# A small load of the output weights split in two: 112 rows, and 16 rows read as 4 groups of 4

## The chip, the core and the metric

The kernel runs on one core of a Trainium2 chip. The metric is the device time of one execution in microseconds (us); the kernel before took 375.05 us, the median of 3 runs (374.96 to 375.16). Besides the compute engines (PE for matmuls, DVE, ACT and POOL for the rest) the core has 16 DMA engines, which move data between the chip's memory and the core's own memory. The compute engines and SP issue loads; the 16 engines carry them out.

## What is computed

One decoding step of attention over a long cache, gated by a small bilinear network:

```python
xn = _layernorm(x, axis=-1)
s = _A_ref(xn, A_k_cache, A_v_cache, A_wq, A_wo)
g = _silu(_B_ref(xn, B_w_gate, B_w_up, B_w_down))
return x + s * g

# _A_ref, cut: 16 query heads share 8 cached heads, 4096 keys of 256, batch 2
scores = jnp.einsum("bhqd,bhkd->bhqk", q, k) * (Dh ** -0.5)
p = _softmax(scores, axis=-1)
o = jnp.einsum("bhqk,bhkd->bhqd", p, v)
return o.reshape(B, Sq, Hq * Dh) @ wo

# _B_ref, cut
h = jnp.einsum("bsd,df->bsf", x, w_gate) * jnp.einsum("bsd,df->bsf", x, w_up)
return jnp.einsum("bsf,fd->bsd", h, w_down)
```

All numbers are 32-bit floats. The caches are 134 MB of the 158.5 MB that are read; each byte is used once.

## The kernel before

The host lays every input out as 128 rows, one for each partition of the core's memory, so that a load is 128 contiguous rows and nothing is rearranged on the way.

**Stages.** First the gating network: `w_gate` and `w_up` come into `low`, `w_down` into `buf1`, `wq` into `buf0`. Then the 16 pairs of cached head and batch follow, two large buffers in turn; each load of the loop (L130) brings 64 KB a partition, the values of one pair beside the keys of the next. The last two pairs' values come as two loads of 32 KB a partition (L133).

**The output weights.** `wo` is 32 steps; a step is a [128, 448] block, 1792 bytes a partition, and is multiplied with a piece of the attention's result (`oT`). The steps come in six loads (L134 to L138): 14, 9 and 4 steps (`ABREAST`) into `low`, then 3, 1 and 1 (`DIRECT`) into the upper half of `buf1`. Each has its own semaphore, `wo0` to `wo5`.

**The order of the loads.** SP issues nearly all loads, one after the other, into one queue (`dma_side`). It waits only until a buffer is free: before L133 until PE is done with a pair, and before the fourth load of `wo` until PE is done with another. What is issued early waits in the queue behind what is in it already. Two small loads are issued by ACT: `x` (2 rows, L162), and `xo`, x again (8 rows, L164).

**The end of the program.** PE waits for each load of `wo` in turn (L438). The first 27 steps accumulate in `o`, four abreast (L322); ACT copies that to `ys` (L196). The last 5 steps go straight to `acc` (L446), and `spread` (L326) adds `ys` to it. Then DVE multiplies with the gate (L295) and adds x (L298), and SP stores the result (L140):

```python
        for n, lo, hi in zip(won, bounds, bounds[1:]):
            e.wait_ge(n, 16)
            for i in range(lo, hi):
```

A load's semaphore reaches 16 when all of its data has landed, so PE goes on when the last of the DMA engines that carry that load is done.

Of the kernel before, what the change touches and what calls it, by code (L numbers as in the profile page):

```python
# [8 lines left out]
B, D = 2, 448  # L9
# [15 lines left out]
WO = 4 * HKV  # L25
ABREAST = (14, 9, 4)
DIRECT = (3, 1, 1)


class Queue:  # L30
# [20 lines left out]
        self.e.wait_ge(sem, n).then_inc(sem, -n)  # L51


def program(nc, known, x, xo, wgu, wd, wq, kv, vv, wo, out):
    def sb(name, shape):
        return nc.alloc_sbuf_tensor(name, shape, F32).ap()

    def ps(name, shape):
        return nc.alloc_psum_tensor(name, shape, F32).ap()

    first = nc.alloc_semaphore("first")
    sems = {n: nc.alloc_semaphore(n) for n in (
        "x", "xg", "gu", "wd", "wq", "k0", "k1", "v14", "v15", "t0", "t1", "pt", "sr", "ob", "q", "m", "mx", "res")}
    won = [nc.alloc_semaphore(f"wo{i}") for i in range(len(ABREAST + DIRECT))]
    pe = Queue(nc, nc.tensor, "pe", known)
    dv = Queue(nc, nc.vector, "dv", known)
# [14 lines left out]
    xg, gate, sig, r0, r1 = (sb(n, [128, SL]) for n in ("xg", "gate", "sig", "r0", "r1"))  # L81
# [8 lines left out]
    m = sb("m", [128, 2])  # L90
    mx = sb("mx", [1, NT, W])
    p = sb("p", [128, 2, 512])
    su = sb("su", [128, 2])
    sr = sb("sr", [128, 128])
    r = [sb(f"r{i}i", [128, REP]) for i in range(2)]
    pT = sb("pT", [128, 2, BLK, 128])
    ob = sb("ob", [128, 512])
# [4 lines left out]
    pt = [ps(f"pt{i}", [128, NK, 128]) for i in range(2)]  # L102
# [5 lines left out]
    bounds = [0]  # L108
    for n in ABREAST + DIRECT:
        bounds.append(bounds[-1] + n)  # L110
    early = bounds[len(ABREAST)]

    def wo_step(i):
        return low[:, i * D:(i + 1) * D] if i < early else late[:, (i - early) * D:(i - early + 1) * D]
# [4 lines left out]
    def dma_side():  # L119
        e = nc.sync  # L120
        for lo, hi in zip(GU, GU[1:]):
            e.dma_start(low[:, lo:hi], wgu[:, lo:hi]).then_inc(sems["gu"], 16)
        e.dma_start(buf[1][:, :14 * D], wd).then_inc(sems["wd"], 16)
        e.dma_start(buf[0][:, :28 * 512], wq).then_inc(sems["wq"], 16)
        sp.after(pe, "y4")
        for h in range(2):
            e.dma_start(buf[1][:, h * ROW:(h + 1) * ROW], kv[0][:, h * ROW:(h + 1) * ROW]).then_inc(sems[f"k{h}"], 16)
        for i in range(N - 2):
            sp.after(pe, *(("q", 1) if i == 0 else ("s", 1) if i == 1 else ("v", i - 2)))
            e.dma_start(buf[i % 2], kv[1 + i]).then_inc(turns[i % 2], 16)  # L130
        sp.after(pe, "v", N - 4)
        for h in range(2):
            e.dma_start(buf[0][:, h * ROW:(h + 1) * ROW], vv[h]).then_inc(sems[f"v{N - 2 + h}"], 16)  # L133
        for n, lo, hi in zip(won, bounds, bounds[1:]):  # L134
            if lo == early:
                sp.after(pe, "v", N - 3)
            t = low[:, lo * D:hi * D] if hi <= early else late[:, (lo - early) * D:(hi - early) * D]
            e.dma_start(t, wo[:, lo * D:hi * D]).then_inc(n, 16)  # L138
        sp.after(dv, "res")
        e.dma_start(out, r1).then_inc(sems["res"], 16)  # L140
        e.wait_ge(sems["res"], 16)
        last = nc.alloc_semaphore("last")
        e.sem_clear(range(first.num, last.num + 1))
# [156 lines left out]
    def pe_side():  # L300
        e = nc.tensor
# [18 lines left out]
        def abreast(t, lhs, rhs, i, total):  # L320
            c = i % NT
            return e.matmul(t[W * c:W * (c + 1), :D], lhs, rhs, start=i < NT, stop=i >= total - NT)  # L322

        def spread(start, stop):
            for c in range(NT):
                ins = e.matmul(acc[W * c:W * (c + 1), :SL], pick.rearrange("p b j -> p (b j)"),  # L326
                               ys[:, c * SL:(c + 1) * SL], start=start, stop=stop)
            return ins
# [104 lines left out]
        def left(i):  # L433
            g, j = divmod(i, 4)
            return oT[g][:, j // 2, j % 2].rearrange("p b j -> p (b j)")

        for n, lo, hi in zip(won, bounds, bounds[1:]):
            e.wait_ge(n, 16)  # L438
            for i in range(lo, hi):
                if i >= 4 * (HKV - 1):  # L440
                    pe.after(dv, "oT", N - 1)
                if i < early:
                    ins = abreast(o, left(i), wo_step(i), i, early)
                else:
                    for c in range(NT):
                        ins = e.matmul(acc[W * c:W * (c + 1), :SL], left(i), wo_step(i)[:, c * SL:(c + 1) * SL],  # L446
                                       start=lo == early and i == lo, stop=i == WO - 1)
            if hi == early:
                pe.ev(ins, "w4")
            if lo == early:  # L450
                pe.after(ac, "accs")
                spread(False, False)
# [3 lines left out]
    act_side()  # L456
    dve_side()
    dma_side()
    pe_side()
    return {q.name: q.at for q in (pe, dv, ac, po, sp)}  # L460

# [44 lines left out]
```

## Time and profile before

| | |
|---|---|
| median of 3 runs | 375.05 us |
| the profiled execution's own time | 375.17 us |
| its span, first instruction to last | 373.9 us |
| PE busy | 243.6 us (65%) |
| DVE, ACT, POOL busy | 60.3, 45.7, 5.0 us |
| mean granted TensorE clock | 0.79 of full speed |

The profile is that of one execution; its times count from the first instruction, and the 1.3 us between span and time lie around it. Busy shares are means over stages. What sets the end is read from the chain of waits, and how evenly the 16 DMA engines are loaded from the DMA share of short windows: it is the mean over the 16, so that a share of 0.50 late in the program is 8 engines at work. A 1/16 is 0.06.

### The profile page before, as it was taken

What the parts mean: (1) busy time and instruction counts of PE and PEld (TensorE: products, weight loads), DVE (VectorE), ACT (ScalarE), POOL (GpSimd) and SP (SyncE); (2) the same over time, 40 slices, a digit from 0 to 9 for tenths busy, and PEclk for the clock granted to TensorE, in tenths of its full rate; (3) what the DMA queues carried; (4) which work ended last, traced back from release to release, by engine and by line L of the source; (5) the groups of instructions that cost most, each with busy time, mean ns of one, the idle gap of its engine ahead of it and who ended that gap; (6) DMA issues with size and microseconds to landing.
All of it is one profiled execution on the core that took longest, in us unless ns stands there. A gap on an engine that the chain in (4) does not pass through costs nothing. (4 is left out here: it accounts for less than half of the span.)

```text
span 373.9 us, 3749 instructions
## 1 busy us (share of the span) xinstructions
PE 243.6 (65%) x1642; PEld 95.1 (25%) x1642; DVE 60.3 (16%) x142; ACT 45.7 (12%) x105; POOL 5.0 (1%) x23
## 2 busy tenths in 40 slices
PE   0093295739393948585776767575758484849786
PEld 0021022322322222323231313122322222232332
DVE  3001002202121212112021203030302020202100
ACT  1002021010102020202020202020202010201110
POOL 1000000000000000000000000000000000000000
PEclk9998588758677687768596859596959586958899
DMA  9999999999999999999999999999999999999995
GB/s 369 400 459 413 430 424 438 444 444 449 449 429 400 435 429 435 449 442 436 407 435 435 435 442 435 449 428 414 435 428 442 442 442 442 400 417 435 417 421 211
DMA packets 4203, 158.70 MB, mean 424 GB/s; under 512 B 610, under 2 KB 868, under 8 KB 1252
## 3 DMA queue, kind: packets, MB, share of 16 engines
q1 hardware_dynamic: 4176, 158.59, 98.4%
q8 instruction: 5, 0.08, 0.1%
q14 instruction: 2, 0.02, 0.0%
q10 hardware_dynamic: 20, 0.01, 0.0%
HBM read 158.54 MB, written 0.06 MB: 424 GB/s over the span
## 5 line engine op out<-in xcount | busy, mean ns | idle before, releaser
L361 PE MATMUL s<-buf,qs 128*32 128x512 f32 x512 | 89.2, 860 | 58.1 <-PEq L51 58.1
L386 PE MATMUL o<-buf,pT 128*32 128x512 f32 x512 | 76.9, 610 | 0.3 <-DVE oT L272 0.3
L178 ACT ACTIVATE p<-s,m 128x512 f32<-128x512 f32 x32 | 21.7, 682 | 251.6 <-DVE m L253 251.6
L361 PEld LDWEIGHTS s<-buf,qs 128*32 128x32 f32 x512 | 22.5, 151 | 111.2 <-issue 111.1
L247 DVE TENSOR_REDUCE m<-s 128x1 f32<-128x1024 f32 x16 | 19.6, 1224 | 144.8 <-PE s L361 144.8
L317 PE MATMUL pt<-ident,p 128*128 128x128 f32 x128 | 22.2, 329 | 12.8 <-PEq L51 12.8
L394 PE MATMUL oc<-sel,ob 128*128 128x2 f32 x128 | 16.4, 250 | 19.8 <-PEq L51 19.8
L386 PEld LDWEIGHTS o<-buf,pT 128*32 128x32 f32 x512 | 17.1, 111 | 32.9 <-issue 30.6
L394 PEld LDWEIGHTS oc<-sel,ob 128*128 128x128 f32 x128 | 15.5, 191 | 33.9 <-issue 33.9
L317 PEld LDWEIGHTS pt<-ident,p 128*128 128x128 f32 x128 | 17.4, 166 | 13.7 <-issue 13.7
L308 PE MATMUL s<-buf,xnT 128*32 128x512 f32 x48 | 7.9, 813 | 10.8 <-DMA buf<-wq 10.8
L308 PE MATMUL s<-low,xnT 128*32 128x448 f32 x48 | 6.5, 692 | 11.9 <-DMA low<-wgu 11.9
L266 DVE COPY pT<-pt 128x512 f32<-128x512 f32 x16 | 11.1, 691 | 18.3 <-PE o L386 17.0
L249 DVE TENSOR_REDUCE mx<-sm 1x128 f32<-1x512 f32 x16 | 10.9, 679 | 10.1 <-PE sm L367 10.1
L192 ACT COPY ob<-o 128x512 f32<-128x512 f32 x16 | 9.3, 582 | 12.5 <-PE o L386 12.5
L183 ACT COPY pT<-pt 128x512 f32<-128x512 f32 x16 | 9.6, 601 | 2.4 <-PE pt L317 2.4
L371 PEld LDWEIGHTS sm<-one,mx 1*128 1x128 f32 x32 | 4.7, 183 | 13.8 <-issue 13.8
L158 POOL COPY qs<-qT 128x64 f32<-128x64 f32 x16 | 3.7, 236 | 293.8 <-PE s L361 243.1
L377 PEld LDWEIGHTS sm<-sel,sr 128*128 128x128 f32 x32 | 7.4, 288 | 0.0
L371 PE MATMUL sm<-one,mx 1*128 1x1 f32 x32 | 6.0, 255 | 1.7 <-PEq L51 1.7
L322 PE MATMUL o<-low,oT 128*32 128x448 f32 x54 | 6.4, 544 | 0.6 <-DMA low<-wo 0.6
L178 ACT ACTIVATION_READ_ACCUMULATOR p<-s,m 128x1 f32 x32 | 6.3, 196 | 0.0
(65 smaller groups left out, 62.4 us busy)
## 6 DMA issues: line engine op xcount, KB each, us to landing
buf<-kv SPq DMA_DIRECT2D x2, 4096.0 KB, 26.1
buf<-vv SPq DMA_DIRECT2D x2, 4096.0 KB, 23.1
buf<-wq SPq DMA_DIRECT2D x1, 7168.0 KB, 41.9
low<-wgu SPq DMA_DIRECT2D x1, 5824.0 KB, 17.0
buf<-wd SPq DMA_DIRECT2D x1, 3136.0 KB, 24.0
low<-wo SPq DMA_DIRECT2D x1, 3136.0 KB, 34.8
low<-wo SPq DMA_DIRECT2D x1, 2016.0 KB, 39.1
low<-wo SPq DMA_DIRECT2D x1, 896.0 KB, 40.9
```

The lines of the kernel that those rows point to most:

```text
L178: ins = e.activation(p[:, h], s[:, h], AF.Exp, bias=m[:, 1:2], scale=1.0 / 16, accum_out=su[:, h:h + 1])
L183: e.copy(pT[:, 1], pt[1]).then_inc(sems["pt"], 1)
L192: e.copy(ob, o).then_inc(sems["ob"], 1)
L247: e.tensor_reduce(m[:, 0:1], s.rearrange("p h n -> p (h n)"), axis=AX.X, op=OP.max).then_inc(sems["m"], 1)
L249: e.tensor_reduce(mx, sm[:1, None, :128].rearrange("p o (c j) -> p o j c", c=NT).to_broadcast([1, NT, W, NT]), axis=AX.X, op=OP.max).then_ ...
L266: e.tensor_copy(pT[:, 0], pt[0]).then_inc(sems["pt"], 1)
L308: e.matmul(t[W * c:W * (c + 1), :n], xnT[:, k, :], block(NT * k + c), start=k == 0, stop=False)
L317: ins = e.transpose(t[:, i, :], a[:, i * 128:(i + 1) * 128], ident)
L361: ins = e.matmul(s[W * c:W * (c + 1), h], qs[i % 2][:, d].rearrange("p j q -> p (j q)"), k[:, h, d, c, :], start=d == 0, stop=d == 1)
L371: pe.ev(e.matmul(sm[:, 128:129], mx.rearrange("p c j -> p (c j)"), one, start=True, stop=True), "x", i)
L386: ins = e.matmul(o[W * at:W * (at + 1), :], pT[:, h, j, 64 * c + 16:64 * c + 48], v[:, h, j, c, :], start=h == 0 and j < 2, stop=h == 1 an ...
L394: ins = e.matmul(oc[:, 2 * d:2 * d + 2], ob[:, h * 256 + d * 128:h * 256 + (d + 1) * 128], sel[:, h], start=h == 0, stop=h == 1)
```

## The change

The third load of `wo` (4 steps, 7168 bytes a row, 128 rows) becomes two. Rows 0 to 111 are loaded from `wo` as before, 112 rows. Rows 112 to 127 come from a new input, `few`, which the host fills with the same numbers: 4 groups, each with 4 rows and a fifth row of zeros that is not read. So the source is 4 groups of 4 rows with a gap behind each, and the target 16 rows of `low`. The new load is issued first, and has a semaphore of its own, for which PE waits after `wo2`.

```diff
+FEW = 4
+MANY = 128 - FEW * FEW
...
             t = low[:, lo * D:hi * D] if hi <= early else late[:, (lo - early) * D:(hi - early) * D]
-            e.dma_start(t, wo[:, lo * D:hi * D]).then_inc(n, 16)
+            if hi == early:
+                e.dma_start(t[MANY:], few[:, :FEW]).then_inc(sems["few"], 16)
+                e.dma_start(t[:MANY], wo[:MANY, lo * D:hi * D]).then_inc(n, 16)
+            else:
+                e.dma_start(t, wo[:, lo * D:hi * D]).then_inc(n, 16)
...
         for n, lo, hi in zip(won, bounds, bounds[1:]):
             e.wait_ge(n, 16)
+            if hi == early:
+                e.wait_ge(sems["few"], 16)
...
+    n = ABREAST[-1] * D
+    few = np.zeros((FEW, FEW + 1, n), wo.dtype)
+    few[:, :FEW] = wo[MANY:, sum(ABREAST) * D - n:sum(ABREAST) * D].reshape(FEW, FEW, n)
```

On SP, at the end of the program, a row is a load, target and source, with its size in rows and numbers. Before:

```order
L133 DMA buf<-vv 128x8192 [waits pe]
L133 DMA buf<-vv 128x8192
L138 DMA low<-wo 128x6272
L138 DMA low<-wo 128x4032
L138 DMA low<-wo 128x1792
L138 DMA buf<-wo 128x1344 [waits pe]
L138 DMA buf<-wo 128x448 x2
```

And now, with all lines of the file some 6 lines further down:

```order
L135 DMA buf<-vv 128x8192 [waits pe]
L135 DMA buf<-vv 128x8192
L144 DMA low<-wo 128x6272
L144 DMA low<-wo 128x4032
L141 DMA low<-few 16x1x1792
L142 DMA low<-wo 112x1792
L144 DMA buf<-wo 128x1344 [waits pe]
L144 DMA buf<-wo 128x448 x2
```

One load more stands between the second and the fourth of `wo`; no other has moved, and none has another wait.

On PE, at the same place, before (L322 is the product with a step of `low`, L446 that with a step of `buf`):

```order
L322 MATMUL o<-low,oT 32x448 [waits wo1]
L322 MATMUL o<-low,oT 32x448 x8
L322 MATMUL o<-low,oT 32x448 [waits wo2]
L322 MATMUL o<-low,oT 32x448 x3
L446 MATMUL acc<-buf,oT 32x112 [waits wo3]
```

And now:

```order
L328 MATMUL o<-low,oT 32x448 [waits wo1]
L328 MATMUL o<-low,oT 32x448 x8
L328 MATMUL o<-low,oT 32x448 [waits few,wo2]
L328 MATMUL o<-low,oT 32x448 x3
L454 MATMUL acc<-buf,oT 32x112 [waits wo3]
```

The matmuls and their order are the same; the first of the 4 steps waits for two semaphores.

More of the change, by code (lines that the diff above doesn't have):

```diff
@@ L51, in take, with program @@
         self.e.wait_ge(sem, n).then_inc(sem, -n)
-def program(nc, known, x, xo, wgu, wd, wq, kv, vv, wo, out):
+def program(nc, known, x, xo, wgu, wd, wq, kv, vv, few, wo, out):
     def sb(name, shape):
@@ L62, in program @@
     sems = {n: nc.alloc_semaphore(n) for n in (
-        "x", "xg", "gu", "wd", "wq", "k0", "k1", "v14", "v15", "t0", "t1", "pt", "sr", "ob", "q", "m", "mx", "res")}
+        "x", "xg", "gu", "wd", "wq", "k0", "k1", "v14", "v15", "t0", "t1", "pt", "sr", "ob", "q", "m", "mx", "res", "few")}
     won = [nc.alloc_semaphore(f"wo{i}") for i in range(len(ABREAST + DIRECT))]
@@ L491 @@
     wd = np.concatenate([full, last], 1).reshape(128, 14 * D)
-    arrays = dict(x=x, xo=xo, wgu=wgu, wd=wd, wq=wq, kv=kv, vv=vv, wo=wo)
+    arrays = dict(x=x, xo=xo, wgu=wgu, wd=wd, wq=wq, kv=kv, vv=vv, few=few, wo=wo)
     def build(known):
```

## The prediction

> **What bounds the kernel now.** I read the page first, its lines on the DMA and its queues:
>
> ```profile
> DMA  9999999999999999999999999999999999999995
> ...
> q1 hardware_dynamic: 4176, 158.59, 98.4%
> q8 instruction: 5, 0.08, 0.1%
> q14 instruction: 2, 0.02, 0.0%
> q10 hardware_dynamic: 20, 0.01, 0.0%
> HBM read 158.54 MB, written 0.06 MB: 424 GB/s over the span
> ```
>
> The 16 DMA engines are busy in every slice but the last, and SP's queue (q1) alone fills 98.4% of their time; PE is busy for 65%. So the kernel is a stream of bytes, and its end is the end of that stream plus a short tail. The chain of waits, asked for the last 19 us, says the same:
>
> ```profile
> 345.57 24.41 DMA buf<-wo
> 369.97 0.04 issue
> 370.01 0.78 PE acc L446 x24
> 370.80 0.19 PE acc L326 x8
> 370.99 0.58 PE acc L446 x16
> 371.57 0.02 issue
> 371.59 0.28 DVE r L295
> 371.88 0.02 issue
> 371.90 0.27 DVE r L298
> ```
>
> Everything hangs on the landing of the last loads of `wo`, at 369.97 us for the fourth. The timeline of PE's weight loads shows who waits there for whom:
>
> ```profile
> 368.40 0.16 PEld L322 LDWEIGHTS o<-low,oT 128*32 128x32 f32 x8 [0.63 <-DMA low<-wo]
> 370.01 0.54 PEld L446 LDWEIGHTS acc<-buf,oT 128*32 128x32 f32 x24 [1.46 <-DMA buf<-wo]
> 370.52 0.23 PEld L326 LDWEIGHTS acc<-ys,pick 128*32 128x32 f32 x8
> 370.71 0.23 PEld L446 LDWEIGHTS acc<-buf,oT 128*32 128x32 f32 x8
> 371.12 0.16 PEld L446 LDWEIGHTS acc<-buf,oT 128*32 128x32 f32 x8 [0.19 <-DMA buf<-wo]
> ```
>
> PE is ahead of the third, the fourth and the last load, and idles before each. So an earlier landing of the last loads ends the program earlier by as much, as long as it is no more than these waits.
>
> A load has landed when its slowest engine is done. How far apart the engines are is read from the DMA share of short windows, the last column but one; times 16 it is the number of engines at work:
>
> ```profile
> core 0: us, PE busy (x) PEld busy (x) DVE busy (x) ACT busy (x) POOL busy (x), PEclk, DMA share, GB/s
> 366.50:368.20 1.70, 1.70 (x18) 0.48 (x10) 0.00 (x0) 0.00 (x0) 0.00 (x0) 1.00 0.98 395
> ...
> 368.95:369.50 0.55, 0.41 (x8) 0.00 (x0) 0.00 (x0) 0.07 (x1) 0.00 (x0) 1.00 0.43 169
> 369.54:369.75 0.21, 0.00 (x0) 0.00 (x0) 0.00 (x0) 0.21 (x1) 0.00 (x0) 1.00 0.40 154
> 369.80:370.12 0.32, 0.10 (x4) 0.11 (x8) 0.00 (x0) 0.16 (x1) 0.00 (x0) 1.00 0.29 112
> 370.15:370.33 0.18, 0.18 (x13) 0.18 (x13) 0.00 (x0) 0.00 (x0) 0.00 (x0) 1.00 0.23 90
> ...
> 370.57:370.64 0.07, 0.07 (x16) 0.07 (x8) 0.00 (x0) 0.00 (x0) 0.00 (x0) 1.00 0.07 26
> 370.66:371.00 0.34, 0.34 (x24) 0.28 (x12) 0.00 (x0) 0.00 (x0) 0.00 (x0) 1.00 0.00 0
> ```
>
> It is a staircase: all 16 to about 368.2, seven (0.43) from 368.95, five (0.29) from 369.80, four (0.23) after 370.15, one (0.07) at 370.6, none after 370.65. Each engine has had the same share of each load. But seven of them fetched instructions besides, as the page's lines of q8 and q14 show, five packets of 16 KB and two of 8 KB. The packet records behind the page's counts (no view lists them, and they name no engine) can be strung into 16 rows, since each begins within 4 ns of the end of the one before; they put one of these seven packets on each of the seven late engines. So nine engines are done by 368.95, up to 1.7 us before the last, and wait for nothing more.
>
> **The change, part by part.** *Moved: bytes between engines.* At 424 GB/s in 98.4% of 16 engines' time, one engine moves 424 / 16 / 0.984 = 26.9 GB/s, so a row of 7168 bytes costs it 0.27 us. Before, each engine carried 8 of the 128 rows. Now the 112 rows give 7 to each, if all 16 serve that load: minus 0.27 us for everyone. The other 16 rows, if 4 engines serve them with a group each, add 4 rows there: in all 11 rows for 8, plus 0.81 us.
>
> How many engines serve the new load is not shown by any row for 4 groups. The nearest is the page's q10, ACT's queue: its two loads have 2 and 8 rows, and 20 packets are 2 + 2 + 8 + 8, a data packet and a count for each row. So 2 rows ran on 2 engines and 8 rows on 8. The bounds for 16 rows in 4 groups are one engine (a load that doesn't divide) and 16; I take 4, since the source is 4 groups that can't be merged, and groups of rows are what q10's loads were dealt by.
>
> [...]
>
> Which four engines they are decides the sign. Of the eight that served the 8-row load, the strung packets end at 368.25, 368.50, 368.84, 368.84, 368.94, 369.52, 369.79 and 370.34. The 2-row load was among these eight too: one of its rows sits on an engine that ended at 368.84, the other most likely on that of 369.52. I assume that the sets are nested, so that the four contain these two and lie in the eight. An engine bears 0.81 us without harm if it ended at 369.57 or before: the last one, at 370.65, now ends 0.27 earlier, at 370.38. Six of the eight are that early.
>
> *Sum, if the four are among the six:* the stream ends at 370.38 for 370.65, minus 0.27 us. The tail follows wholly: PE's waits before the last loads (0.63, 1.46 and 0.19 us above) are waits for these same landings, so PE starts earlier by 0.27 at each. What would be late next is ACT's copy of `o` to `ys`, for which `spread` waits:
>
> ```profile
> 369.43 0.53 ACT L196 COPY ys<-o 128x448 f32<-128x448 f32 x1 [8.17 <-PE o L322]
> ```
>
> It ends at 369.96, and L326 starts at 370.61; both move by 0.27, so 0.65 us of cover stay.
>
> *Added: one load on SP.* It is issued at about 327.4, and behind it SP waits anyway, as the waits of SP's queue and the timeline show:
>
> ```profile
> SPq L138 <- PE o L386: 17.7, 1, 17.7
> ...
> 326.50 1.38 SPq L138 DMA_DIRECT2D low<-wo  x3
> 345.57 1.28 SPq L138 DMA_DIRECT2D buf<-wo  x3
> ```
>
> Three issues take 1.38 us, so one more is about 0.46 us in a wait of 17.7 us: nothing. Without that cover it would delay the three loads of L138 behind it, and they wait in the queue until 368 in any case. In the stream the load adds four small count packets to four engines; bounded by nothing and by the 0.04 us that the chain gives to an issue, I take nothing.
>
> *Added: one wait on PE* before the 4 steps at 368.40. Behind it stand these steps, ACT's copy and `spread`. The new load is ahead of the 112 rows in every engine's queue, so its count is there first; the instruction lies in the 0.63 us that PE waits for `wo2`. Without that cover its price is between nothing and 0.04 us. I take nothing. That both instructions could shift the fetch of instructions is open to either side; bounds are none and one late engine more or less, and as six others end after 369.5, I take none.
>
> The sum against the profiled execution: 375.17 - 0.27 = 374.90. The median of the runs is 0.12 below that execution; on it the sum gives **374.78 us**, minus 0.07%.
>
> **The rivals.** *One of the four is the engine of 369.79.* It then ends at 370.60, 0.05 before the old end: 375.05 - 0.05 = 375.0. For it: that engine is one of the six from which two places are still to be filled. Against: the four early ones fill them as well.
>
> *One of the four is the engine of 370.34.* It ends at 371.15, 0.50 later than the last one now; 375.55. The same for and against.
>
> *The other side: the 16 rows run on a single engine,* because 16 rows and 4 groups are not dealt out as I think. Then it carries 23 rows for 8, plus 15 x 0.27 = 4.05 us, and ends at 372.3 to 374.4 for an engine that ended at 368.25 to 370.34: plus 1.65 to 3.7 us, 376.7 to 378.8 us. It decides as soon as the rows added cost more than that engine's slack of 0.3 to 2.4 us; two engines (plus 7 rows, 1.9 us) would stand near the point. Against it: ACT's loads ran on as many engines as rows.
>
> *Each load pays a price of its own in the stream.* The nearest row is the store of the result, alone in the queue, from issue to landing:
>
> ```profile
> res<-r SPq DMA_DIRECT2D x1, 56.0 KB, 1.6
> ```
>
> If the third load's place cost that much again, 376.65. Against it: between the landing of the fourth load at 369.97 and PE's start on the sixth at 371.12 lie two whole loads, in 1.15 us; a queue that is full hides what a lone load shows. It decides only if the queue runs empty between loads.
>
> [...]
>
> **How the numbers follow.** Four among the six early ones, 374.8: 0.46. With the engine of 369.79 but not 370.34, 375.0: 0.20. With the engine of 370.34, 375.55: 0.24 (it is one of about five for two places, less since nothing else moves). One engine, or a price for each load, 376.65 and more: 0.07. Something that gives more than the one row that is shed: 0.03. The range takes in the first three with the runs' own spread of 0.1 to 0.2 us, **374.5 to 375.7**. About 0.2%, 0.75 us, is what a measurement of this kernel can tell from no change; the first three all lie within it, 0.90 together, of which 0.02 goes to slower, since the third is only 0.25 us from that bound. So the same 0.88, slower 0.09, faster 0.03.
>
> **What would show it.** In the windows of the end: the last engine done at 370.4 for 370.65, and about ten at work around 369.2 for seven. The fourth load would end at 369.7 in the chain for 369.97, and PE's wait before 371.12 would move to about 370.85. The page's q1 tells the number of engines: its 4176 packets are 29 loads of 128 rows and 16 counts; 4 engines for the new load make it 4180, one 4177, sixteen 4192. I am wrong if the stairs end later than before, if the new load is carried by another number of engines, or if the fetches of instructions sit on other engines than before.

## The result, and the profile after

The changed kernel takes 378.05 us, the median of 6 runs (377.83 to 378.28), against 375.12 us before in the same comparison: a ratio of 1.0078, 95% interval 1.0065 to 1.0091. It is 2.9 us slower; 374.8 was forecast, with a range up to 375.7.

The page of the changed kernel, its lines on the DMA and its queues:

```profile
DMA  9999999999999998999999999999999999999995
...
q1 hardware_dynamic: 4180, 158.59, 98.5%
...
HBM read 158.54 MB, written 0.06 MB: 421 GB/s over the span
```

The 4180 packets are the 4 more that were reckoned with if 4 engines serve the new load. So the count is what the forecast deal of the rows would give, and the engines are as busy as before, but they move less: 421 GB/s over the span for 424. The chain of waits of the changed kernel, from 355 us on:

```profile
345.68 27.05 DMA buf<-wo
372.74 0.04 issue
372.78 0.78 PE acc L454 x24
373.56 0.19 PE acc L332 x8
373.75 0.60 PE acc L454 x16
374.35 0.02 issue
374.38 0.29 DVE r L301
374.66 0.02 issue
374.69 0.28 DVE r L304
```

The fourth load of `wo` lands at 372.74 us for 369.97, 2.77 us later; behind it the tail is what it was. So nearly all of the loss lies ahead of that landing. The timeline of PE's weight loads says from which load on:

```profile
362.53 0.16 PEld L328 LDWEIGHTS o<-low,oT 128*32 128x32 f32 x8
...
367.66 0.16 PEld L328 LDWEIGHTS o<-low,oT 128*32 128x32 f32 x8 [2.74 <-DMA low<-wo]
...
371.41 0.16 PEld L328 LDWEIGHTS o<-low,oT 128*32 128x32 f32 x8 [2.11 <-DMA low<-wo]
372.78 0.54 PEld L454 LDWEIGHTS acc<-buf,oT 128*32 128x32 f32 x24 [1.21 <-DMA buf<-wo]
```

The second load, which the change doesn't touch, is already late: PE starts on it at 367.66. In the kernel before it starts at 366.13:

```profile
366.13 0.16 PEld L322 LDWEIGHTS o<-low,oT 128*32 128x32 f32 x8 [1.37 <-DMA low<-wo]
```

On the split one it starts at 371.41 for 368.40. The windows of one microsecond show what the DMA engines did meanwhile; the last two columns are their share and what they moved. A packet is counted whole in the window in which it starts, so that a share can pass 1. First the kernel before, then the changed one:

```profile
364.00:365.00 1.00, 1.00 (x14) 0.25 (x7) 0.00 (x0) 0.00 (x0) 0.00 (x0) 1.00 1.03 430
365.00:366.00 1.00, 0.56 (x4) 0.00 (x0) 0.00 (x0) 0.00 (x0) 0.00 (x0) 1.00 0.91 364
366.00:367.00 1.00, 0.87 (x12) 0.38 (x16) 0.00 (x0) 0.00 (x0) 0.00 (x0) 1.00 1.00 401
367.00:368.00 1.00, 1.00 (x13) 0.26 (x6) 0.00 (x0) 0.00 (x0) 0.00 (x0) 1.00 1.00 401
```

```profile
362.00:363.00 1.00, 1.00 (x14) 0.74 (x17) 0.23 (x1) 0.00 (x0) 0.00 (x0) 1.00 1.06 452
364.00:365.00 1.00, 1.00 (x14) 0.36 (x8) 0.00 (x0) 0.00 (x0) 0.00 (x0) 1.00 1.09 253
365.00:366.00 1.00, 0.73 (x4) 0.00 (x0) 0.00 (x0) 0.00 (x0) 0.00 (x0) 1.00 1.09 222
366.00:367.00 1.00, 0.00 (x0) 0.00 (x0) 0.00 (x0) 0.00 (x0) 0.00 (x0) 1.00 0.89 190
367.00:368.00 1.00, 0.33 (x4) 0.16 (x8) 0.00 (x0) 0.00 (x0) 0.00 (x0) 1.00 1.18 226
368.00:369.00 1.00, 1.00 (x16) 0.37 (x9) 0.00 (x0) 0.00 (x0) 0.00 (x0) 1.00 0.85 188
369.00:370.00 1.00, 1.00 (x7) 0.11 (x1) 0.00 (x0) 0.00 (x0) 0.00 (x0) 1.00 0.96 235
370.00:371.00 1.00, 0.11 (x1) 0.00 (x0) 0.00 (x0) 0.00 (x0) 0.00 (x0) 1.00 0.95 278
```

A share near 1 at little more than half the bytes: no engine is idle, and a packet takes almost twice as long in the mean. Over the 7 us from 364 on, 1.59 MB were moved (the sum of the seven rows); at the 421 GB/s of the whole span it would have been 2.95 MB. The 1.36 MB that are missing are 3.2 us of the stream, by this estimate, which is the loss and some more. Packet by packet the records say the same: one of 7168 bytes took 0.28 us in the mean before and 0.51 us after.

So the question is what makes all packets slow while the split load is in flight.

### The profile page after: what moved, and what is told of

Read it like the earlier page. It is cut to its first block, busy times and chain, and to the rows that moved or that the text cites. A ratio compares the mean times of both kernels' runs of the same rounds, so it can differ in the third digit from the quotient of the medians.

```text
span 376.7 us, 3751 instructions
## 1 busy us (share of the span) xinstructions
PE 243.8 (65%) x1642; PEld 96.2 (26%) x1642; DVE 60.4 (16%) x142; ACT 45.7 (12%) x105; POOL 5.0 (1%) x23
## 3 DMA queue, kind: packets, MB, share of 16 engines
q1 hardware_dynamic: 4180, 158.59, 98.5%
## 5 line engine op out<-in xcount | busy, mean ns | idle before, releaser
L367 PE MATMUL s<-buf,qs 128*32 128x512 f32 x512 | 87.0, 841 | 58.9 <-PEq L53 58.9
L323 PE MATMUL pt<-ident,p 128*128 128x128 f32 x128 | 23.7, 346 | 12.8 <-PEq L53 12.8
L323 PEld LDWEIGHTS pt<-ident,p 128*128 128x128 f32 x128 | 18.6, 175 | 13.7 <-issue 13.7
```

The lines of the kernel that those rows point to most:

```text
L323: ins = e.transpose(t[:, i, :], a[:, i * 128:(i + 1) * 128], ident)
L367: ins = e.matmul(s[W * c:W * (c + 1), h], qs[i % 2][:, d].rearrange("p j q -> p (j q)"), k[:, h, d, c, :], start=d == 0, stop=d == 1)
```

## The experiments

Four theories. **PLACE**: the rows of a full load of 128 are dealt to the engines in a way in which they don't disturb each other, and the new loads deal them otherwise. **FEW**: the load in groups is what slows the others. **OVERLOAD**: nothing is slow but the four engines with 11 rows. **SOURCE**: the rows are read in an order that the memory serves badly. In a first round, each kernel is the changed one with one thing else in it.

**few_beside**: the small load kept, the large one whole.

```diff
+    spare = sb("spare", [128, 1664])
...
-                e.dma_start(t[MANY:], few[:, :FEW]).then_inc(sems["few"], 16)
-                e.dma_start(t[:MANY], wo[:MANY, lo * D:hi * D]).then_inc(n, 16)
+                e.dma_start(spare[MANY:], few[:, :FEW, :1664]).then_inc(sems["few"], 16)
+                e.dma_start(t, wo[:, lo * D:hi * D]).then_inc(n, 16)
```

> The third load of wo is one load of 128 rows again, as before; the 16 rows of few (6656 bytes of each row) are loaded besides, by the same 4 groups of 4, to a spare place that nothing reads. Bytes are added, none taken away. Theory PLACE (the 112-row load deals rows to the 16 engines so that they write into each other's part of the core's memory, and all packets slow down while it is in flight): without the 112 rows packets of 7168 bytes take 0.27 us again; four engines carry 4 x 0.25 = 1.0 us more; about as before, 375.0 to 375.9. Theory FEW (the load of 4 groups is what slows the others): slow as the change, about 378. Theory OVERLOAD (four engines with more rows set the end): about 376 to 378.

376.73 us, ratio 1.0046 (1.0029 to 1.0063). It is above what PLACE said, less than FEW said, and within the range of OVERLOAD. The 16 rows by themselves cost 1.65 us; their 106 KB, spread over all engines, would be 0.25 us at 421 GB/s. So PLACE as it stood, with the 112 rows alone to blame, has missed here.

**rows16_even**: the large load as changed, the other 16 rows taken plainly.

```diff
-                e.dma_start(t[MANY:], few[:, :FEW]).then_inc(sems["few"], 16)
+                e.dma_start(t[MANY:], wo[MANY:, lo * D:hi * D]).then_inc(sems["few"], 16)
```

> The 112-row load stays as in the change; the other 16 rows come straight from wo as one load of 16 rows, so that every engine should get one. All engines carry equal bytes again. Theory PLACE: still slow, 377.5 to 378.5, and packets of 7168 bytes take about 0.5 us. Theory FEW and theory OVERLOAD: back to before, 375.0 to 375.3.

378.32 us, ratio 1.0084 (1.0067 to 1.0101). Without a load in groups it is as slow as the change. Every engine carries equal bytes in it if the 16 rows go to 16 engines, an estimate from q10's 20 packets, by which 2 and 8 rows went to 2 and 8. By that OVERLOAD falls as the cause, and FEW as the only cause. The windows of this kernel show the same half rate:

```profile
364.00:365.00 1.00, 1.00 (x12) 0.19 (x4) 0.00 (x0) 0.00 (x0) 0.00 (x0) 1.00 1.14 203
...
368.00:369.00 1.00, 1.00 (x16) 0.29 (x9) 0.00 (x0) 0.00 (x0) 0.00 (x0) 1.00 0.86 199
```

**groups16x8**: one load of 128 rows, but in 16 groups of 8 neighbouring rows, meant for an engine each. The diff is against the kernel before; there is no second wait.

```diff
-            e.dma_start(t, wo[:, lo * D:hi * D]).then_inc(n, 16)
+            if hi == early:
+                e.dma_start(t, few[:, :8]).then_inc(n, 16)
+            else:
+                e.dma_start(t, wo[:, lo * D:hi * D]).then_inc(n, 16)
...
+    n = ABREAST[-1] * D
+    few = np.zeros((16, 9, n), wo.dtype)
+    few[:, :8] = wo[:, sum(ABREAST) * D - n:sum(ABREAST) * D].reshape(16, 8, n)
```

> One load of 128 rows, as before, but its source is 16 groups of 8 rows with a gap behind each group, so that an engine should get 8 neighbouring rows; all engines carry equal bytes, and there is no second load. Theory PLACE: which engine writes which rows is what matters; slow, 376.5 to 379, packets of 7168 bytes at about 0.5 us. Theories FEW, OVERLOAD: as before, 375.0 to 375.3. Theory SOURCE (the 112 rows are read from memory in an order that makes reads slow): open, the source is other than in the change.

380.19 us, ratio 1.0120 (1.0086 to 1.0154): slow without any split, and the packets of the load took 0.56 us in the mean. The median is above the expected range, its fastest run, 378.44, within it; in its profiled execution PE's clock fell to 0.50 at the end besides (last section).

**packed112**: as rows16_even, from an input in which the rows lie side by side.

```diff
-                e.dma_start(t[MANY:], few[:, :FEW]).then_inc(sems["few"], 16)
-                e.dma_start(t[:MANY], wo[:MANY, lo * D:hi * D]).then_inc(n, 16)
+                e.dma_start(t[MANY:], few[MANY:]).then_inc(sems["few"], 16)
+                e.dma_start(t[:MANY], few[:MANY]).then_inc(n, 16)
...
-    few = np.zeros((FEW, FEW + 1, n), wo.dtype)
-    few[:, :FEW] = wo[MANY:, sum(ABREAST) * D - n:sum(ABREAST) * D].reshape(FEW, FEW, n)
+    few = c(wo[:, sum(ABREAST) * D - n:sum(ABREAST) * D])
```

> 112 rows and 16 rows, both read from a new input that holds these 4 steps alone, so that the rows lie next to each other in memory, 7168 bytes apart and no longer 57344. Where they are written is as in rows16_even. Theory PLACE: as slow as rows16_even, 377.5 to 378.5. Theory SOURCE (the distance of rows in memory): back to before, 375.0 to 375.3.

378.45 us, ratio 1.0098 (1.0077 to 1.0118). The distance of the rows in memory is not it.

What the four can have in common is that engines write other rows of the core's memory than in a full load. No trace names the engine of a packet, so which rows an engine writes in a full load is not shown. What can be varied is the target: few_beside with the small load written to another place, and nothing else changed in the kernel.

**few_rows0**, **few_rows16**, **few_rows64**: the same load to three places. The diff takes few_rows0 against few_beside; the others have `spare[16:32]` and `spare[64:80]`.

```diff
-                e.dma_start(spare[MANY:], few[:, :FEW, :1664]).then_inc(sems["few"], 16)
+                e.dma_start(spare[0:16], few[:, :FEW, :1664]).then_inc(sems["few"], 16)
```

> As few_beside (one load of 128 rows as before, and the 16 short rows of few loaded besides to a spare place that nothing reads), but few is written to rows 0 to 15 of the spare place and no longer to rows 112 to 127. Source, groups, engines and bytes are the same. [...] Theory FORM (a load with 4 groups, or on 4 engines, slows everything wherever it writes): 376.4 to 377.0, as few_beside.

> As few_rows0, with rows 16 to 31 as target. [...] Theory FORM: 376.4 to 377.0 too. A rival within PLACE, that only the upper half or the last rows are bad: as before, 375.0 to 375.4.

> [...] The rival that only rows 112 to 127 are bad: 375.0 to 375.4.

To rows 0 to 15: 375.26 us, ratio 1.0006 (0.9996 to 1.0016). That is 0.26 us above the kernel before in the same comparison, about what the added bytes are worth, and the interval takes in no change. To rows 16 to 31: 376.58 us, 1.0050 (1.0030 to 1.0070). To rows 64 to 79: 376.57 us, 1.0038 (1.0024 to 1.0053). Source, groups and bytes are the same in all, and the order of the loads; the target, the only thing that the kernels change, is worth 1.3 us. FORM falls, and so does the rival that only the upper half or the last rows are bad; OVERLOAD and SOURCE don't explain few_beside either: few_rows0 loads the same rows from the same source for 0.26 us. By the packet records the 16 packets of 6656 bytes took 0.26 us in the mean to rows 0 to 15, 0.43 us to rows 16 to 31 and 0.44 us to rows 64 to 79. Rows at which the small load costs more than its bytes are called foreign from here on: 16 to 31 and 64 to 79, and 112 to 127 by few_beside. Rows 0 to 15 are not; other places were not tried. What makes rows foreign, no trace shows; that it is the engine that writes them in a full load is the author's guess. The windows of few_rows0, and then of few_rows64:

```profile
364.00:365.00 1.00, 0.75 (x6) 0.00 (x0) 0.00 (x0) 0.00 (x0) 0.00 (x0) 1.00 1.06 443
365.00:366.00 1.00, 0.00 (x0) 0.00 (x0) 0.00 (x0) 0.00 (x0) 0.00 (x0) 1.00 0.89 368
366.00:367.00 1.00, 0.77 (x8) 0.29 (x12) 0.00 (x0) 0.00 (x0) 0.00 (x0) 1.00 1.01 416
```

```profile
364.00:365.00 1.00, 1.00 (x12) 0.23 (x4) 0.00 (x0) 0.00 (x0) 0.00 (x0) 1.00 1.30 324
365.00:366.00 1.00, 0.42 (x4) 0.00 (x0) 0.00 (x0) 0.00 (x0) 0.00 (x0) 1.00 0.77 160
366.00:367.00 1.00, 0.00 (x0) 0.00 (x0) 0.00 (x0) 0.00 (x0) 0.00 (x0) 1.00 1.12 262
...
368.00:369.00 1.00, 1.00 (x13) 0.23 (x3) 0.00 (x0) 0.00 (x0) 0.00 (x0) 1.00 1.00 412
```

In the three microseconds from 364 on few_rows0 moves 1227 KB and few_rows64 746 KB. The 481 KB between them are 1.15 us at 420 GB/s, of the 1.3 us by which it is slower. Then the rate is back: 412 GB/s from 368 on.

**few2_rows64**: two groups of 4 rows in place of four; the diff is against few_rows64.

```diff
-                e.dma_start(spare[64:80], few[:, :FEW, :1664]).then_inc(sems["few"], 16)
+                e.dma_start(spare[64:72], few[:2, :FEW, :1664]).then_inc(sems["few"], 16)
```

> [...]

375.92 us, ratio 1.0026 (1.0017 to 1.0035): 0.66 us above few_rows0, half of what the four groups cost there. Whether the two engines that carry the two groups (an engine for each is an estimate, as before) are slowed alone or others with them, the time doesn't say. The rate decides:

```profile
364.00:365.00 1.00, 0.64 (x4) 0.00 (x0) 0.00 (x0) 0.00 (x0) 0.00 (x0) 1.00 1.18 394
365.00:366.00 1.00, 0.00 (x0) 0.00 (x0) 0.00 (x0) 0.00 (x0) 0.00 (x0) 1.00 0.91 200
366.00:367.00 1.00, 0.01 (x2) 0.01 (x2) 0.00 (x0) 0.00 (x0) 0.00 (x0) 1.00 0.89 332
```

200 GB/s from 365 to 366 us. In the same window few_rows0 moved 368; if two of the 16 engines had stood still and the others kept their rate, 14/16 of that would be left, 322. So by that estimate others are slowed too: 8 foreign rows nearly halve the rate of the whole stream, only for a shorter time. The packet records say the same: every data packet that starts between 365.00 and 365.75 takes 1.8 to 2.7 times as long as one of its size does in the kernel before. The profiled execution took 376.94 us, 1.0 above the median, since PE's granted clock fell in it from 368 on (0.50 from 369 to 371), behind the stretch that is read here (last section).

Three runs tried the sum by itself; each leaves out a part of `wo`. **two_steps_less** takes bytes from a full load, more than the change does; the diff is against the kernel before:

```diff
-            e.dma_start(t, wo[:, lo * D:hi * D]).then_inc(n, 16)
+            cut = 2 * D if hi == early else 0
+            e.dma_start(t[:, :(hi - lo) * D - cut], wo[:, lo * D:hi * D - cut]).then_inc(n, 16)
```

> The kernel before, but the third load of wo brings only 2 of its 4 steps, still in 128 rows; the last two of the 27 steps are computed with what stood there before. Tests a term of the prediction's sum by itself: 3584 bytes a row less are 8 x 3584 = 28.7 KB for each engine, 1.07 us at 26.9 GB/s; if the tail follows wholly, 375.1 - 1.07 = 374.0. If something else holds the end, less than that.

374.26 us, ratio 0.9981 (0.9971 to 0.9990): 0.74 us less, not 1.07. The chain of waits of this kernel shows why:

```profile
362.89 6.23 PE o L323 x54
369.11 0.02 issue
369.14 0.54 ACT ys L197
369.68 0.04 issue
369.72 0.40 PE acc L327 x8
```

No load ends last any more, but PE's 27 steps and ACT's copy behind them: PE works without a gap from 362.89 us on. So the loads can be earlier than that is worth. The gain is near the cover of 0.65 us that the prediction named between ACT's copy and `spread`. The landing itself moved as the sum says: from PE's first weights of the second load to those of the fourth it is 2.80 us (365.90 to 368.70), for 3.88 us before (366.13 to 370.01), 1.08 us less for 1.07.

**one_row_less** (`cut = D // 2`, the 7168 bytes for each engine that the change sheds) and **shed_and_own** (the same, and the 16 rows of few to rows 0 to 15 of the spare place besides):

> The shed alone: the third load 896 bytes a row short (half of the last of the 27 steps is computed with what stood there before), nothing added. 7168 bytes less for each engine, 0.27 us: 374.7 to 374.9 by the prediction's sum; if ACT's copy or PE already holds the tail, 375.0.

> The case that the prediction reckoned with, without foreign rows: the third load of wo is one load of 128 rows, but 896 bytes a row short (half of the last of the 27 steps is computed with what stood there before), which takes 7168 bytes from every engine; and 4 engines get 4 rows of 6656 bytes each besides, to rows 0 to 15 of a spare place. Theory PLACE: packets at full speed, the last engine ends 0.27 us earlier, 374.7 to 374.9. If the prediction's sum was wrong in another term too (the tail doesn't follow, or the four engines now end last), 375.0 to 375.6.

374.78 us, ratio 0.9994 (0.9985 to 1.0003), and 374.92 us, 0.9995 (0.9986 to 1.0004). The first median lies in the expected range and the second just above it; both intervals take in no change. The landings, in one profiled execution of each, agree with the sum: the fourth load ends at 369.67 and at 369.64 in their chains, for 369.97.

```profile
346.06 23.60 DMA buf<-wo
369.67 0.04 issue
```

```profile
345.79 23.85 DMA buf<-wo
369.64 0.04 issue
```

No version with the whole of `wo` was found that beats the kernel before. The 0.27 us need four engines to take over rows of others, and no run shows that done without the slowing.

## Why the prediction was wrong

**The step that failed** is "*Moved: bytes between engines*": "one engine moves 424 / 16 / 0.984 = 26.9 GB/s, so a row of 7168 bytes costs it 0.27 us". That rate was read where every load was a full one, and was used for loads of another shape. In the changed kernel a row of the 112 costs 0.51 us in the mean, and the stream is slow for as long as the 112 rows and the 16 are in flight. The term "minus 0.27 us for everyone" took it for granted that a row costs the same wherever an engine writes it. What stands in its place is a rate that depends on the target: 1.3 us between few_rows0 and few_rows16, which differ in nothing else. Of the 2.9 us, no part needs the load in groups: with the 16 rows taken plainly it is as slow (rows16_even, 378.32). The load of 4 groups is worth 1.65 us beside a whole load (few_beside). The 112 rows without any other load were not run, so how the two parts share the loss is open. That the 112 rows are slow for the same reason as the 16 is not shown. It fits rows16_even, packed112 and groups16x8 (378.32, 378.45 and 380.19 us); the target alone was varied for the small load only.

**What held.** That the stream of bytes bounds the kernel, and that the tail follows the last landing: it moved by 2.77 us, and from it to the end are 3.96 us for 3.93. That 4 engines serve the load in groups and 16 that of 112 rows: the 4180 packets agree with it. The staircase at the end and the engines with slack: written to rows 0 to 15, 4 groups of 4 rows more cost 0.26 us, within the interval of no change (few_rows0). The shed of 0.27 us: landings 0.30 and 0.33 us earlier, in one execution each. Nothing, or little, for the issue on SP and the wait on PE: few_rows0 has both in its 0.26 us.

**Which engines.** In the packet records of few_beside and of few_rows0 two of the four engines carry a fetch of 8 KB and two carry none, which points to the second case, with the engine of 369.79 and a gain of 0.05, and not to the likeliest one. The stringing is not unique, so this is not shown. Between the two cases lie 0.2 us; it didn't matter.

**Where a small thing was wrong.** "Both move by 0.27, so 0.65 us of cover stay": ACT's copy does not move. The prediction read PE's waits from the weight loads; the matmuls of all 13 steps behind the second load's landing run as one piece, so the third load is not what they wait for:

```profile
366.13 3.23 PE L322 MATMUL o<-low,oT 128*32 128x448 f32 x26 [0.57 <-DMA low<-wo]
```

Of the cover 0.38 us would have stayed. two_steps_less shows where it ends.

**The rivals.** None had this mechanism. "Each load pays a price of its own", 376.65, was nearest by its number and wrong by its reason: few_rows0 has a load more and pays 0.26 us, where its bytes are worth 0.25. "A single engine", also on that side, is refuted by the packets. The other side got 0.09, worked out from mishaps in the dealing of bytes; that a load in flight could slow all others wasn't asked, though no row of before showed a load of other than 128 rows at a size that counts.

## What to carry to other kernels

On a stream that fills all 16 DMA engines, load whole sets of 128 rows, and cut columns rather than rows (one_row_less: a landing 0.30 us earlier): here the loads of 112 and of 16 rows slowed everything in flight beside them to about half (188 to 278 GB/s for 421 over the span), and even 16 rows of 6.5 KB, to foreign rows, did so for a microsecond (160 GB/s in few_rows64). Evening out engines by moving rows cost 2.9 us here, where 0.27 was to be had. And a rate read from loads of one shape is a rate for that shape; a new shape needs its own bound, and the DMA share beside the GB/s of the same window shows at once which of the two has changed.

## What the runs showed of the hardware

Foreign rows slow the whole stream and not, by the estimate above, only the engines that carry them: 200 GB/s at a share of 0.91 with two groups of foreign rows (few2_rows64), for 368 at 0.89 in the same microsecond of few_rows0; 188 to 278 GB/s from 364 to 371 us in the changed kernel. Why all are slowed stays open; the runs only show when.

The second finding is PE's clock. In the profiled execution of rows16_even the tail's same 48 matmuls ran at a granted clock of 0.51, the last column but two, after PE had waited for data; in that of the changed kernel it was 1.00:

```profile
372.80:375.40 2.60, 2.47 (x48) 2.07 (x48) 0.00 (x0) 0.00 (x0) 0.00 (x0) 0.51 0.05 21
```

```profile
372.70:374.40 1.70, 1.53 (x48) 1.08 (x48) 0.02 (x1) 0.27 (x1) 0.00 (x0) 1.00 0.12 45
```

2.47 us of work for 1.53, about 0.9 us more. The profiled executions of groups16x8 and few2_rows64 show the same half (0.50 from 375.0 to 377.6 us and from 369 to 371). So a late load may cost twice: by the wait, and by the clock after it; no run varied the wait alone. PE waited 2.27 us for the second load in rows16_even, and 1.94 us in the changed kernel, where the clock stayed at full to the end of PE's work. In the clock records of the kernel before and of the changed one every whole stretch at one granted clock is 3.41 us or a multiple of it, up to 20.5 us (the last at half: 349.28 to 352.70 us before, 349.70 to 353.12 in the changed kernel). Whether the length of a wait decides, or the moment at which it falls, was not tried.
